# Layer one of a feed-forward block as seven block products instead of eight, on one Trainium2 core

## The chip, the cores and the metric

The kernel runs on one core of one Trainium2 chip. The metric is the device time of one execution in microseconds, as the median of the runs listed below. Five engines of the core work side by side: TensorE (PE in the profile; its weight loads are shown as PEld), VectorE (DVE), ScalarE (ACT), GpSimd (POOL) and SyncE (SP), which here issues every DMA.

## The reference

Attention over 8 sequences with 8 heads (32 global tokens and 512 local ones per sequence, head size 64), then layer norm and a feed-forward block with a residual. Cut to what matters:

```python
# out_g: every global query sees all keys
# out_l: a local query sees 32 keys to either side and the global keys
x = concatenate([out_g, out_l], axis=2).transpose(0, 2, 1, 3).reshape(8, 544, 512)
mu, var = mean(x), mean((x - mu) ** 2)            # over the last axis
xn = (x - mu) / sqrt(var + 1e-6) * g_ln
out = x + maximum(xn @ w_ch1, 0.0) @ w_ch2        # w_ch1: 512 x 2048, w_ch2: 2048 x 512
```

All inputs are fp32 (the weights are given as float64). The kernel gets fp32 accuracy out of matmuls on a rounded format, fp32r, by splitting each operand into a high part and a low rest, and adding three products: low by high, high by low, high by high.

## The kernel before

The 4352 tokens are worked in nine chunks. Chunks 0 to 7 hold 512 local tokens each (two halves of 256 tokens, each a half of one sequence), chunk 8 the 256 global tokens. Within a chunk the feed-forward block runs over 16 row tiles `f` of 128 hidden units each:

- `hidden(f)` (L804) is layer one of a row tile: three products times four contraction tiles `kt` of 128, so 12 matmuls of 512 columns, all into one PSUM bank `ph`.
- `relu` (L815, ACT) writes the high part `hh` out of `ph`, `rest` (L819, DVE) the low part `hl`.
- `out(f, t)` (L831) is layer two: for each of four token tiles `t` three matmuls of 512 columns, added up in PSUM over all 16 row tiles (`acc`). The outputs of row tile `f` stand behind `hidden(f + 1)`. At the end of a chunk DVE adds the residual (L863) and SP stores (L864).

The split weights of all 16 row tiles, high and low, of both layers, stay in SBUF from chunk 0 on (`wts`).

The attention of later chunks is put between these matmuls. `attend(u, before)` issues the scores of one pair of heads `u` (L454), the values of the pair before (L522), the masked row maxima (L472, DVE), the exponentials (L487, ACT), and turns the 32x32 blocks of the result on DVE (L413). `PAIR_PLACES` and `GLOBAL_PLACES` say behind which half row tile each piece starts. The pieces are generators in a queue `side`; each call of `step()` between two groups of matmuls moves the first one on to its next `yield`. What is issued so is in the fixed order of each engine's queue: nothing overtakes anything on its engine. After the last pair of a half of a chunk, DVE takes the statistics (L236), GpSimd the power (L243), ACT normalises (L252), DVE turns the tokens (L413), and `split_chunk` scales them by `g_ln` into high parts (L761, ACT) and low rests (L763, DVE).

GpSimd has little to do behind chunk 0: for each attention pair an addition and a power on 8 columns (L534, L536), for each half the norm's power.

Of the kernel before, what the change touches and what calls it, by code (L numbers as in the profile page):

```python
# [21 lines left out]
P = 128  # L22
# [48 lines left out]
PAIR_PLACES = (4, 10, 18, 24)  # L71
GLOBAL_PLACES = (1, 7, 20)
# [3 lines left out]
REBIAS = 2.0 ** -112  # L76
HUGE = 122877.9921875 * REBIAS
# [6 lines left out]
def attention_ffn_kernel(  # L84
# [82 lines left out]
    wts = {}  # L167
# [3 lines left out]
    class Weights:  # L171
# [42 lines left out]

        def high(self):
            w = wpool.tile([P, 2, KT * P + DM], F32R, name="w", tag=f"w{self.f}")
            wts[self.f] = w[:, 0], w[:, 1]
            nc.scalar.copy(w[:, 0], self.tmp)  # L218

        def low(self):  # L220
            hi, lo = wts[self.f]
            nc.vector.tensor_tensor(lo, self.tmp, f32(hi), op=ALU.subtract)  # L222

    class Norm:
# [46 lines left out]
        def steps(self):  # L271
            self.stats()
            self.power()
            yield
            self.shift()
# [7 lines left out]
    def new_x():  # L283
        return fpool.tile([P, 2, DM], F32, name="x", tag=next(xtags))
# [135 lines left out]
    class Pair:  # L420
# [135 lines left out]
        def norm(self):  # L556
            half = self.at[2]
            xn = ready.setdefault(self.chunk, [None, None])[half] = new_x()
            return Norm(token_tile(self.chunk, half), range(2), xn)

    class Global:
# [39 lines left out]
        def reduce(self, part):  # L601
            if part == 0:
                self.p = fpool.tile([P, 2, SA], F32, name="gp", tag="ob")
# [34 lines left out]
        def turns(self, half):  # L638
# [4 lines left out]
            for n in range(4 * half, 4 * half + 4):  # L643
                turn_blocks(p, self.pt, n)
                yield
# [94 lines left out]
    def split_chunk(xns, turns, out):  # L740

        def source(h, kt):
            if h in turns:
                return turns[h].rearrange("p j (k q) -> p j k q", k=KT)[:, :, kt]
            t = ps_a.tile([P, 512], F32, name="t", tag="att")
            for j in range(2):
                at = slice(j * P, (j + 1) * P)
                nc.tensor.transpose(t[:, at], xns[h][:, j, kt * P:(kt + 1) * P], ident)
            return t[:, :256].rearrange("p (j q) -> p j q", j=2)

        for kt in range(KT):
            planes(kt, out, len(xns) > 1)
            parts = [
                (source(h, kt), *(
                    a[:, h * 256:(h + 1) * 256].rearrange("p (j q) -> p j q", j=2) for a in out[kt]
                ))
                for h in range(len(xns))
            ]
            g = g_sb[:, kt:kt + 1]
            for t, hi, lo in parts:  # L760
                nc.scalar.activation(hi, t, AF.Copy, scale=g)  # L761
            for t, hi, lo in parts:
# [488 lines left out]
```

## Time and profile before

| | |
|---|---|
| median of 3 runs | 899.88 us (898.98 to 900.23) |
| profiled execution, its own time | 898.62 us |
| its span, first to last instruction | 896.8 us |
| TensorE busy | 880.2 us (98%) |
| VectorE busy | 626.0 us (70%) |
| ScalarE busy | 301.6 us (34%) |
| GpSimd busy | 112.7 us (13%) |
| DMA moved | 119.28 MB, mean 133 GB/s |

Busy times are sums over the span. The profiled execution takes 1.8 us more than its span, and 1.3 us less than the median of the runs.

### The profile page before, as it was taken

Reading aid. Unit: us, or ns where it says so; the run is one execution under the profiler, and the core shown is the slowest. Engines: PE = TensorE matmul, PEld = TensorE weight load, DVE = VectorE, ACT = ScalarE, POOL = GpSimd, SP = SyncE. Lnnn points to the kernel's source line nnn. Section 1 sums busy time; section 2 is a strip of 40 time slices with the busy share of each in tenths; the row PEclk is TensorE's granted clock in tenths of the full one; section 3 lists DMA queues with packets and bytes.
Section 4 is the critical chain, followed back from the end, with each engine's and each line's share of the span. In section 5 each row is a group of like instructions: output and inputs, shape, how many; then the busy total and the mean of one; then the engine's idle time right before and its main releaser. Section 6 shows DMA issues by size and latency. Waiting matters only on the chain.

```text
span 896.8 us, 20638 instructions
## 1 busy us (share of the span) xinstructions
PE 880.2 (98%) x8492; PEld 702.7 (78%) x8492; DVE 626.0 (70%) x1765; ACT 301.6 (34%) x843; POOL 112.7 (13%) x152
## 2 busy tenths in 40 slices
PE   6899999999999999999999999999999999999998
PEld 4777777788777887788877887878877787777897
DVE  6886835878868786787958786888958775342611
ACT  7876754323233233323232232323332212111211
POOL 5731221101011000111011000010011000000000
PEclk9999999999999999999999999999999999999999
DMA  9992448323253243423253243423263123302100
GB/s 352 417 419 72 164 127 302 126 74 122 109 187 102 79 149 126 157 64 128 108 211 102 80 148 104 157 74 125 103 232 102 48 72 99 120 0 63 50 21 23
DMA packets 48109, 119.28 MB, mean 133 GB/s; under 512 B 4240, under 2 KB 15504, under 8 KB 44944
## 3 DMA queue, kind: packets, MB, share of 16 engines
q1 hardware_dynamic: 48016, 117.98, 37.3%
q8 instruction: 66, 1.08, 0.5%
q14 instruction: 27, 0.22, 0.1%
HBM read 100.14 MB, written 17.83 MB: 132 GB/s over the span
## 4 chain that ended last, share of the span: by engine, by line
PE 91%; DMA 5%; ACT 1%; DVE 1%; SPq 0%; issue 0%; ACTq 0%
PE ph L804 41%; PE acc L831 41%; DMA raw<-in_wd 3%; PE sc L454 3%; PE pv L522 3%; DMA u<-in_eu 2%; PE gsc L653 1%; PE gsc L591 1%; DVE w L222 1%; ACT p L487 0%; PE pv L653 0%; PE tp L502 0%; DVE tmp L211 0%; ACT w L218 0%; PE t L700 0%
## 5 line engine op out<-in xcount | busy, mean ns | idle before, releaser
L831 PE MATMUL acc<-w,hh 128*128 128x512 f32 x1088 | 342.2, 396 | 0.0
L804 PE MATMUL ph<-xh,w 128*128 128x512 f32 (+1 forms) x1240 | 310.4, 377 | 1.5 <-DVE hl L819 1.5
L804 PEld LDWEIGHTS ph<-xh,w 128*128 128x128 f32 x1240 | 216.5, 188 | 49.2 <-DVE hl L819 2.5
L831 PEld LDWEIGHTS acc<-w,hh 128*128 128x128 f32 x1088 | 204.8, 188 | 48.2
L815 ACT ACTIVATE hh<-ph 128x512 fp32r<-128x512 f32 (+1 forms) x147 | 83.2, 566 | 438.4 <-PE ph L804 433.4
L831 PE MATMUL acc<-w,hl 128*128 128x512 f32 x544 | 216.9, 399 | 0.0
L819 DVE SCALAR_TENSOR_TENSOR hl<-ph,hh 128x512 fp32r<-128x512 f32 (+1 forms) x147 | 95.6, 651 | 164.9 <-ACT hh L815 163.4
L413 DVE STREAM_TRANSPOSE pt<-p 32x256 f32<-32x256 f32 x368 | 160.3, 435 | 5.2
L804 PE MATMUL ph<-xl,w 128*128 128x512 f32 (+1 forms) x524 | 141.1, 391 | 0.0
L831 PEld LDWEIGHTS acc<-w,hl 128*128 128x128 f32 x544 | 102.1, 188 | 24.1 <-issue 0.6
L487 ACT ACTIVATE p<-p,mn 128x128 f32<-128x128 f32 x224 | 87.3, 391 | 93.2 <-DVE mn L472 89.8
L804 PEld LDWEIGHTS ph<-xl,w 128*128 128x128 f32 x524 | 97.3, 188 | 23.1
L413 DVE STREAM_TRANSPOSE x<-x 32x256 f32<-32x256 f32 x208 | 90.7, 436 | 6.2 <-ACT x L252 3.2
L472 DVE CUSTOM_DVE_ANT_0 p<-sc,mask 128x128 f32<-128x128 f32 x224 | 51.2, 286 | 49.2 <-PE sc L454 49.2
L413 DVE STREAM_TRANSPOSE gpt<-gp 32x256 f32<-32x256 f32 x128 | 55.5, 434 | 1.8
L536 POOL TENSOR_TENSOR ri<-ri,powers 128x8 f32<-128x8 f32 x29 | 49.8, 1716 | 2.4
L487 ACT ACTIVATION_READ_ACCUMULATOR p<-p,mn 128x1 f32 x224 | 41.9, 187 | 0.0
L242 POOL TENSOR_SCALAR rs<-mv 128x2 f32<-128x2 f32 x17 | 4.8, 281 | 258.6 <-DVE mv L238 258.5
L534 POOL TENSOR_SCALAR ri<-sm 128x8 f32<-128x8 f32 x29 | 7.4, 256 | 205.1 <-ACT p L487 204.2
L454 PEld LDWEIGHTS sc<-e 64*32 64x32 f32 x1792 | 24.9, 105 | 9.8 <-issue 9.2
L454 PE MATMUL sc<-e 64*32 64x128 f32 x1792 | 32.4, 274 | 0.0
L522 PEld LDWEIGHTS pv<-v,pt 128*32 128x32 f32 x1792 | 26.3, 110 | 6.0 <-issue 6.0
(90 smaller groups left out, 523.9 us busy)
## 6 DMA issues: line engine op xcount, KB each, us to landing
v<-in_eu SPq DMA_DIRECT2D x28, 1024.0 KB, 7.3
e<-in_eu SPq DMA_DIRECT2D x28, 672.0 KB, 8.1
raw<-in_wd SPq DMA_DIRECT2D x16, 1024.0 KB, 15.5
gk<-in_gk SPq DMA_DIRECT2D x8, 1088.0 KB, 8.0
ob<-xs SPq DMA_DIRECT2D x34, 256.0 KB, 7.1
out<-ob SPq DMA_DIRECT2D x34, 256.0 KB, 2.2
xs<-x SPq DMA_DIRECT2D x32, 256.0 KB, 8.6
gv<-in_gv SPq DMA_DIRECT2D x16, 512.0 KB, 4.4
```

Source lines behind the costliest of these rows:

```text
L222: nc.vector.tensor_tensor(lo, self.tmp, f32(hi), op=ALU.subtract)
L413: nc.vector.transpose(out=to[rp][..., gp], in_=a[gp][..., rp])
L454: nc.tensor.matmul(sc[h][gp, at:at + P], self.e[hd, j, w * WIN:(w + 1) * WIN], self.e[hd, j, k0 * WIN:(k0 + 4) * WIN], start=True, stop=Tr ...
L472: nc.vector.tensor_tensor_reduce(out=self.p[:, j, c], in0=self.sc[h][:, at:at + P], in1=masks[self.at[2], qb], scale=-QSCALE, scalar=BIG, ...
L487: nc.scalar.activation(self.p[:, j, c], self.p[:, j, c], AF.Exp, bias=self.mn[:, j, c:c + 1], scale=-1.0, accum_out=self.sm[:, j, c:c + 1],)
L522: nc.tensor.matmul(self.pv[gp, at:at + D], self.pt[:, j, 2 * h + qb, gp], self.v[:, j, 4 * qb + g, h * D:(h + 1) * D], start=True, stop=Tr ...
L536: nc.gpsimd.tensor_tensor(ri, ri, minus_one.to_broadcast([P, 8]), op=ALU.pow)
L591: nc.tensor.matmul(banks[h][i * SG:(i + 1) * SG, :c1 - c0], self.q[h * D:(h + 1) * D, i, :], self.k[h * D:(h + 1) * D, i, c0:c1], start=Tr ...
L804: nc.tensor.matmul(ph[:, :n], w[:, kt, :], xx[kt][:, part.start:part.start + n], start=(i == 0), stop=(i == 3 * KT - 1),)
L815: nc.scalar.activation(hh[:, :n], self.ph[f, start][:, :n], AF.Relu)
L819: nc.vector.scalar_tensor_tensor(hl[:, :n], self.ph[f, start][:, :n], 0.0, f32(hh[:, :n]), ALU.max, ALU.subtract)
L831: nc.tensor.matmul(self.acc[t], a[:, ts], w, start=(f == 0 and i == 0), stop=(f == NF - 1 and i == 2),)
```

## The change

For chunks 2 to 7, layer one of two neighbouring row tiles (a pair `p` of row tiles: 256 hidden units) is made by seven block products in place of eight. The weights of the pair are cut into 2x2 blocks (128 hidden units by 256 contraction rows), the tokens into 2x2 blocks (256 contraction rows by 256 tokens). Sums and differences of weight blocks and of token blocks take the place of some blocks, and the four result blocks are sums of products. Layer two is computed as before.

- `Sums.sums`, `high`, `low` and `store`, run by `prepare` during chunk 1: GpSimd makes four sums of weight blocks for each of the 8 pairs, ACT and GpSimd split them into high and low, and SP stores all eight blocks of each pair to a DRAM tile `wb` (`Weights.store` the plain ones). `prepare` is moved on once at each of four places per row tile of chunk 1; it has 53 steps.
- `load_blocks(p, True)` loads the seven blocks of a pair back, for each pair of each chunk, in four DMAs, into places that the layer-one weights of row tiles 0 to 7 held; pairs with even numbers have one set of places, odd ones the other. The blocks of pair `p + 2` are loaded as soon as pair `p` has used its own. Chunk 8 loads the four plain blocks of a pair (`load_blocks(p, False)`).
- `pair` replaces two calls of `hidden`: 42 matmuls of 256 columns into three half banks `x`, `y` and `w`. A running sum stays in `x`: product 2 is added to product 0 there, then 4, then 6. Between them ACT copies the partial sums out (`s1`, `s7`, `s6`, `s2`, `s5`, `s4`), GpSimd adds pairs of these copies, and `relu` and `rest` follow for four blocks, three of the rests on GpSimd. The layer-two matmuls of the pair before stand between the products and behind them: `FILLS` gives one token tile ahead of products 2, 4 and 6 each, and five follow product 6.
- The last layer-two outputs of a chunk are carried into the next chunk's first pair (`carried`).
- `turn_half` scales the turned tokens by `g_ln` (ACT), `token_sums` makes four sums of token blocks (GpSimd), and `split_blocks` splits seven token blocks of 128x512 into high (ACT) and low (DVE). They take the place of `split_chunk`.
- The attention pairs move to other places, and their GpSimd power is issued behind their own exponentials; the two halves of a pair's row maxima are issued together.

The first chunk keeps its order, chunk 1 keeps `hidden`. The diff, cut:

```diff
-PAIR_PLACES = (4, 10, 18, 24)
-GLOBAL_PLACES = (1, 7, 20)
+FILLS = (0, 0, 1, 0, 1, 0, 1)
+STAGE_AT = 4
+PAIR_PLACES = ((2, 8, 15, 21), (2, 7, 14, 18, 30), (6, 14, 18, 30))
+GLOBAL_PLACES = ((29, 31, 31), (22, 31, 31))
...
+        def sums(self):
+            pool, tag = ((apool, "gk"), (fpool, "ob"))[self.p % 2]
+            ab = apool.tile([P, 2, KT * P], F32, name="wf", tag="gp")
+            for i in range(2):
+                w = f32(wide[2 * self.p + i][:, :, :KT * P])
+                nc.gpsimd.tensor_tensor(ab[:, i], w[:, 0], w[:, 1], op=ALU.add)
+                yield
+            a, b = ab[:, 0], ab[:, 1]
+            self.s = pool.tile([P, 4, 2, KH], F32R, name="ws", tag=tag)
+            self.lo = f32(self.s[:, :, 1])
+            for n, (i, x, y, op) in enumerate((
+                (2, b[:, :KH], b[:, KH:], ALU.add),
+                (1, self.lo[:, 2], a[:, :KH], ALU.subtract),
+                (0, a[:, :KH], b[:, :KH], ALU.subtract),
+                (3, a[:, KH:], self.lo[:, 1], ALU.subtract),
+            )):
+                nc.gpsimd.tensor_tensor(self.lo[:, i], x, y, op=op)
...
+    def load_blocks(p, seven):
+        for n, at in enumerate(
+            (slice(0, 2), slice(2, 4), slice(4, 6), slice(6, 7)) if seven
+            else (slice(0, 4, 3), slice(5, 8, 2))
+        ):
+            blocks = wb[p][at].rearrange("b p l c -> p b (l c)")
+            nc.sync.dma_start(
+                f32(wide[p % 2 * 4 + n])[:, :blocks.shape[1], :KT * P], blocks
+            )
...
+        for n, a, b in (
+            (0, x[0, 1], x[0, 0]), (2, x[1, 1], x[0, 1]), (1, x[1, 1], t[0]), (3, x[1, 0], t[1]),
+        ):
+            nc.gpsimd.tensor_tensor(t[n], a, b, op=ALU.subtract)
+            yield
...
+        for n, a in enumerate((x[0, 0], t[2], t[1], x[1, 0], t[0], t[3], x[1, 1])):
...
+            nc.scalar.copy(as_block(hi), a)
+            nc.vector.tensor_tensor(as_block(lo), a, as_block(f32(hi)), op=ALU.subtract)
...
+        def pair(self, p, fill):
...
+            def product(i, to, start=True, stop=True):
+                a, b = block_at(p, i), self.xt[i]
+                for n, (l, r) in enumerate(((a[1], b[0]), (a[0], b[1]), (a[0], b[0]))):
+                    for k in range(KB):
+                        nc.tensor.matmul(
+                            to, l[:, k * P:(k + 1) * P], r[:, k * KH:(k + 1) * KH],
...
+            fill(0)
+            product(0, x, stop=False)
+            nc.scalar.copy(s1, x)
+            fill(1)
+            product(1, w, stop=False)
+            nc.scalar.copy(s7, w)
+            fill(2)
+            product(2, x, False, False)
+            nc.scalar.copy(s6, x)
+            fill(3)
+            product(3, y, False, False)
+            nc.scalar.copy(s2, y)
+            add(s1, s2)
+            fill(4)
+            product(4, x, False, False)
+            nc.scalar.copy(s5, x)
+            add(s5, s7)
+            fill(5)
+            product(5, w, False)
+            nc.scalar.copy(s4, w)
+            add(s6, s4)
+            relu(0, 0, s1)
+            rest_pool(0, 0, s1)
+            fill(6)
+            product(6, x, False)
+            relu(0, 1, x)
+            rest(0, 1, x)
+            relu(1, 1, s5)
+            rest_pool(1, 1, s5)
+            relu(1, 0, s6)
+            rest_pool(1, 0, s6)
+            fill(7)
...
+        for kt in range(KT):
+            nc.scalar.activation(x[:, :, kt], x[:, :, kt], AF.Copy, scale=g_sb[:, kt:kt + 1])
+            if kt % 2:
                 yield
+        if len(halves) == 2:
+            yield from token_sums(u.chunk)
+            summed.add(u.chunk)
```

How the change moves instructions is shown at three places. First TensorE, in the middle of chunk 5. Before, a row tile of layer one (`ph`, 12 matmuls) and behind it the first of the four token tiles of layer two of the row tile before (`acc`):

```order
L804 MATMUL ph<-xh_6328,w 128x512 x2
L804 MATMUL ph<-xh_6344,w 128x512 x2
L804 MATMUL ph<-xl_6329,w 128x512 x2
L804 MATMUL ph<-xl_6345,w 128x512 x2
L804 MATMUL ph<-xh_6328,w 128x512 x2
L804 MATMUL ph<-xh_6344,w 128x512 x2
L831 MATMUL acc_6498<-w,hl 128x512
L831 MATMUL acc_6498<-w,hh 128x512 x2
```

And in the changed kernel, pair 3 of chunk 5, with an attention pair (`sc`, `pv`) behind it:

```order
L1031 MATMUL ph<-xb,w 128x256 x6
L1031 MATMUL ph<-w 128x256 x6
L956 MATMUL acc_7603<-w 128x512 x3
L1031 MATMUL ph<-w 128x256 x6
L1031 MATMUL ph<-xb,w 128x256 x6
L956 MATMUL acc_7622<-w 128x512 x3
L1031 MATMUL ph<-w 128x256 x12
L956 MATMUL acc_7645<-w 128x512 x3
L1031 MATMUL ph<-w 128x256 x6
L528 MATMUL sc<-e 32x128 x32
L596 MATMUL pv<-v,pt_7778 32x64 x32
```

Two row tiles of layer one, 24 matmuls of 512 columns, have become seven products of six matmuls of 256 columns, and three of the eight layer-two tiles of the pair before stand between them. Over the whole program 1152 matmuls of 512 columns are gone and 2016 of 256 columns are there instead; the 1632 of layer two stay.

Second ScalarE, the same part of a chunk. Before, exponentials (`p`), the ReLU that makes `hh`, and the normalisation (`x<-x,rs`):

```order
L815 ACTIVATE hh<-ph 128x512 x3
L487 ACTIVATE p_6800,sm_6805<-p_6800,mn_6799 128x128 x8
L815 ACTIVATE hh<-ph 128x512
L252 ACTIVATE x<-x,rs 128x512 x2
L815 ACTIVATE hh<-ph 128x512 x3
```

And in the changed kernel, around one pair of row tiles that follows an attention pair (`sn` are the copied sums, `w` here the places that take the high part of the hidden units, `x<-x,g_sb` the scaling of turned tokens):

```order
L561 ACTIVATE p_8068,sm_8073<-p_8068,mn_8067 128x128 x8
L1055 COPY sn<-ph 128x256
L1058 COPY sn<-ph 128x256
L1061 COPY sn<-ph 128x256
L1254 ACTIVATE x<-x,g_sb 128x2x128 x2
L1064 COPY sn<-ph 128x256
L1254 ACTIVATE x<-x,g_sb 128x2x128 x2
L1068 COPY sn<-ph 128x256
L1072 COPY sn<-ph 128x256
L1039 ACTIVATE w<-sn 128x256
L1039 ACTIVATE w<-ph 128x256
L1039 ACTIVATE w<-sn 128x256 x2
```

Where two ReLUs of 512 columns stood, there are now six copies and four ReLUs of 256 columns, and other work of ScalarE stands between the copies.

Third GpSimd, the start of chunk 1. Before, the power of an attention pair and little else:

```order
L534 TENSOR_SCALAR ri_1826<-sm_1812 128x8
L536 TENSOR_TENSOR ri_1826<-ri_1826,powers 128x8
L630 TENSOR_SCALAR gsm<-gsm 128x2
L534 TENSOR_SCALAR ri_2116<-sm_1812 128x8
L536 TENSOR_TENSOR ri_2116<-ri_2116,powers 128x8
```

In the changed kernel (`wf` are whole weights, high plus low, `ws` the four sums of a pair):

```order
L248 TENSOR_TENSOR wf<-w 128x512 x2
L259 TENSOR_TENSOR ws<-wf 128x256
L259 TENSOR_TENSOR ws<-ws,wf 128x256
L259 TENSOR_TENSOR ws<-wf 128x256
L259 TENSOR_TENSOR ws<-wf,ws 128x256
L248 TENSOR_TENSOR wf<-w 128x512 x2
L608 TENSOR_SCALAR ri_2091<-sm_2070 128x8
L610 TENSOR_TENSOR ri_2091<-ri_2091,powers 128x8
L269 TENSOR_TENSOR ws<-ws 128x2x256
```

Each of the 8 pairs brings two additions of 512 columns, four sums of 256 and two subtractions of 512 to GpSimd in chunk 1.

## Rows read from the trace of the kernel before

**Rows 1.** The page: span, and busy time of each engine.

```profile
span 896.8 us, 20638 instructions
PE 880.2 (98%) x8492; PEld 702.7 (78%) x8492; DVE 626.0 (70%) x1765; ACT 301.6 (34%) x843; POOL 112.7 (13%) x152
```

**Rows 2.** The page: chain that ended last, share of the span by engine.

```profile
PE 91%; DMA 5%; ACT 1%; DVE 1%; SPq 0%; issue 0%; ACTq 0%
```

**Rows 3.** Windows: stretch, length, busy us of PE PEld DVE ACT POOL, PEclk, DMA share, GB/s.

```profile
230.00:330.00 100.00, 100.00 (x1003) 79.52 (x1002) 78.71 (x230) 30.62 (x96) 9.75 (x13) 1.00 0.36 125
```

**Rows 4.** Waits of the whole span: who waited for whom, us, times, longest.

```profile
ACT hh L815 <- PE ph L804: 433.4, 127, 7.6
...
PE ph L804 <- DVE hl L819: 1.5, 2, 0.8
```

**Rows 5.** The chain in order of time, chunk ends: start us, us, what.

```profile
339.41 5.62 PE acc L831 x24
...
441.03 5.62 PE acc L831 x24
```

**Rows 6.** Timeline, weight loads in chunk 3: start us, us, what.

```profile
407.50 0.89 PEld L804 LDWEIGHTS ph<-xh,w 128*128 128x128 f32 x4
...
410.31 0.19 PEld L831 LDWEIGHTS acc<-w,hl 128*128 128x128 f32 x1
...
413.12 0.89 PEld L804 LDWEIGHTS ph<-xh,w 128*128 128x128 f32 x4
```

**Rows 7.** Timeline, start of chunk 8, whose layer one has 256 columns.

```profile
846.97 3.06 PEld L804 LDWEIGHTS ph<-xh,w 128*128 128x128 f32 x24
847.20 3.04 PE L804 MATMUL ph<-xh,w 128*128 128x256 f32 x24
...
850.08 0.39 PE L831 MATMUL acc<-w,hl 128*128 128x512 f32 x1
...
850.28 0.39 ACT L815 ACTIVATE hh<-ph 128x256 fp32r<-128x256 f32 x1 [1.06 <-PE ph L804]
```

**Rows 8.** Groups by line and form: count, busy us, mean ns, idle before.

```profile
L815 ACT ACTIVATE hh<-ph 128x512 fp32r<-128x512 f32 x125 | 74.9, 599 | 395.7 <-PE ph L804 390.7 <-PE acc L831 4.7
...
L252 ACT ACTIVATE x<-x,rs 128x512 f32<-128x512 f32 x30 | 22.8, 809 | 13.4 <-DVE rs L246 13.4
...
L761 ACT ACTIVATE xh<-x,g_sb 128x256 fp32r<-128x256 f32 x52 | 21.5, 498 | 0.0
...
L815 ACT ACTIVATE hh<-ph 128x256 fp32r<-128x256 f32 x22 | 8.3, 383 | 42.7 <-PE ph L804 42.7
```

**Rows 9.** Groups of GpSimd by line and form.

```profile
L536 POOL TENSOR_TENSOR ri<-ri,powers 128x8 f32<-128x8 f32 x29 | 49.8, 1716 | 2.4
L197 POOL TENSOR_SCALAR raw<-raw 128x1024 int32<-128x1024 uint16 x5 | 16.7, 3342 | 9.7 <-DMA raw<-in_wd 9.4
...
L534 POOL TENSOR_SCALAR ri<-sm 128x8 f32<-128x8 f32 x29 | 7.4, 256 | 205.1 <-ACT p L487 204.2
...
L200 POOL TENSOR_SCALAR tmp<-tmp 128x1024 f32<-128x1024 f32 x2 | 2.1, 1068 | 8.1 <-ACT tmp L185 8.1
```

**Rows 10.** Windows of 4 us in which the DMA engines were nearly full.

```profile
258.00:262.00 4.00, 4.00 (x18) 3.21 (x18) 1.98 (x8) 2.01 (x9) 1.91 (x2) 1.00 1.00 389
...
322.00:326.00 4.00, 4.00 (x19) 3.24 (x18) 3.37 (x10) 2.51 (x6) 0.94 (x2) 1.00 0.94 295
```

**Rows 11.** DMA issues of the page: KB each, median us from issue to landing.

```profile
v<-in_eu SPq DMA_DIRECT2D x28, 1024.0 KB, 7.3
e<-in_eu SPq DMA_DIRECT2D x28, 672.0 KB, 8.1
```

**Rows 12.** Timeline of an attention pair of chunk 3.

```profile
399.91 1.16 PE L454 MATMUL sc<-e 64*32 64x128 f32 x64
...
401.44 0.40 ACT L487 ACTIVATE p<-p,mn 128x128 f32<-128x128 f32 x1 [3.62 <-DVE mn L472]
...
404.70 0.19 ACT L487 ACTIVATION_READ_ACCUMULATOR p<-p,mn 128x1 f32 x1
```

More of the change, by code (lines that the diff above doesn't have):

```diff
@@ L764, in split_chunk, with step @@
             yield
     out_flat = out.rearrange("b s d -> (b s) d")
-    side, first = deque(), deque()
-    def step():
-        for queue in (first, side):
-            while queue:
-                if next(queue[0], queue) is not queue:
+    side, ends, later = deque(), deque(), deque()
+    held = {}
+    def step(free=1, queues=(side, later, ends)):
+        for queue in queues:
+            while queue and held.get(queue[0], 0) <= free:
+                got = next(queue[0], queue)
+                if got == "wait":
+                    break
+                if got is not queue:
+                    held[queue[0]] = got or 0
@@ L893, in attention_ffn_kernel @@
     weights = [Weights(f) for f in range(NF)]
+    sums = [Sums(p) for p in range(NP)]
     ready, tokens = {}, {}
@@ L896, in attention_ffn_kernel @@
     halves_turned = {}
+    summed = set()
     def token_tile(c, half):
         if (c, half) not in tokens:
-            tokens[c, half] = new_x()
+            tokens[c, half] = new_x((c, "token"))
         return tokens[c, half]
@@ L904, in attention_ffn_kernel, with prepare, attend @@
     acm, apool = open_pool("apool")
-    def accumulators():
-        return [ps_o.tile([P, 512], F32, name="gsc", tag=f"acc{t}") for t in range(4)]
-    def attend(u, before):
+    def prepare():
+        for p in range(NP + 1):
+            s, before = sums[p] if p < NP else None, sums[p - 1] if p else None
+            steps = s.sums() if s else iter(())
+            for n in range(4):
+                if n % 2 == 0 and before:
+                    before.high(n // 2)
+                next(steps, None)
+                yield
+                if n % 2 and before:
+                    before.low(n // 2)
+                    yield
+            if p:
+                before.store()
+            if p == NP - 1:
+                globals_[0].load_scores()
+            for w in weights[2 * p:2 * p + 2]:
+                w.store()
+        yield
+    def attend(u, before, late=False):
         if u:
@@ L916, in attend @@
             before.values()
-            before.sums()
             if before.next:
@@ L966, in attend_global @@
+    def attend_global(g, before, tag="gq"):
+        g.scores(0, [ps_a.tile([P, 512], F32, name="sc", tag="att") for _ in range(2)])
+        banks = [ps_h.tile([P, 512], F32, name="gsc", tag="ph") for _ in range(2)]
+        before.values(banks[0][:, P:2 * P])
+        g.scores(1, banks)
         g.reduce(0)
         g.reduce(1)
-        if before:
-            before.output()
+        before.output(tag)
         g.load_values()
-        if g.next:
-            g.next.load_scores()
+        yield
+        for h in range(2):
+            g.exps(h)
+            yield
@@ L973, in attend_global, with first_global @@
+    def first_global(g):
+        g.scores(0, [ps_a.tile([P, 512], F32, name="sc", tag="att") for _ in range(2)])
+        yield
+        g.scores(1, [ps_h.tile([P, 512], F32, name="gsc", tag="ph") for _ in range(2)])
+        g.reduce(0)
+        g.reduce(1)
+        g.load_values()
         yield
```

392 lines of the change are left out of this document (279 added, 113 removed).

## The prediction

> **What bounds the kernel now.** The page's busy shares come first: TensorE is busy in 880.2 of 896.8 us [rows 1]. That alone proves little, since ends of matmuls are modelled, so the chain that ended last is read next: 91% of the span lies on TensorE, 5% on DMA (the start) [rows 2]. The window of 100 us in the middle shows no idle TensorE at a granted clock of 1.00, that is 2.4 GHz, while VectorE works 78.7, ScalarE 30.6 and GpSimd 9.8 us and the DMA engines are filled to 0.36 [rows 3]. The waits agree: ScalarE waits 433 us for layer one, TensorE in layer one 1.5 us for others [rows 4]. So from chunk 1 on the time is the sum of what TensorE issues, and 101.6 us per chunk (339.41 to 441.03) [rows 5]. Fewer matmul columns shorten the run, as long as nobody else gets late.
>
> **TensorE's part.** The pace of a matmul is read from start to start. Twelve loads of 512-column matmuls go from 407.50 to 410.31, the next twelve to 413.12: 2.81 us each, 0.234 per matmul [rows 6]. In chunk 8 layer one already has 256 columns: 24 matmuls from 847.20 to 850.08, 0.120 each [rows 7]. A pair of row tiles took 24 x 0.234 = 5.62 us and takes 42 x 0.120 = 5.04, so 0.58 less; 48 pairs (8 in each of chunks 2 to 7) give 27.8 us. The work in multiplications falls by an eighth, the time by a tenth, since a matmul of 256 columns costs more than half of one of 512. Bounds: below, half of 0.234, 0.117, which gives 4.92 and 33.8 us in all; above, the loads' own row, 3.06 us for 24, 0.1275 each [rows 7], which gives 5.36 and 12.8 us. I take 0.120, a start-to-start time of the same shape, with the loads in that stretch back to back. The gain is gone at 5.62 / 42 = 0.134.
>
> In that stretch the weight loads have no gap (3.06 us of loads within 2.99 us, 846.97 to the next block's) [rows 7]. The Trainium skill, "TensorE: Matmul & The Clock Gate", section "LDWEIGHTS (loading the stationary operand)", has a load take its columns divided by 1.2 ns, 107 ns for 128. By that alone, as an estimate, a pair would take 4.5 us and the run about 848; the row's 0.120 is 12% slower, and I follow the row.
>
> **The chain within a pair.** A product takes 0.72 us, a layer-two tile 3 x 0.234 = 0.70, a pair of row tiles 7 x 0.72 + 8 x 0.70 = 10.64. Products 0, 2, 4 and 6 go into the same bank, and each must wait until ScalarE has copied the sum before. From the end of a 256-column group (850.08, the next starts) to ScalarE's start are 0.20 us, and it works 0.39 [rows 7]: a copy is done 0.59 behind its product. Between products 0 and 2 stand product 1 and a tile, 1.42 us; between 2 and 4, and 4 and 6, likewise. So each has 0.83 us to spare. The first pair of a chunk has no tile ahead of product 6, there 0.13 are left. What eats the spare time is what stands between the copies on ScalarE. Scaling by g costs 0.498 a piece [rows 8]: with two behind s6 and two behind s2, counted from product 2's end, the copies end at 0.59 (s6), 1.98 (s2) and 3.36 (s5), and product 6 wants s5 at 3.56. With four behind s2, s5 ends near 3.7, 0.1 late. A normalisation (0.809) stands behind s5, where nobody waits soon. The eight exponentials behind an attention pair run from 401.44 to 404.89, that is from 1.5 to 5.0 us after the scores began (399.91) [rows 12]; the next first copy is due more than 6 us after the scores begin (2.1 of attention, five tiles of 3.5, one product), so they fit. I book 0.3 us per chunk for such misses, and 1 us for the handover from chunk 1, together 3 us.
>
> **ScalarE and VectorE in sum.** A pair brings ten ScalarE operations of 0.39 for two of 0.60 [rows 8], 2.7 us more, 22 us per chunk on top of 30.6; scaling and casts of tokens add about 4. That is 57 of 97 us. VectorE loses three of four rests. Neither becomes the bound.
>
> **GpSimd.** No row shows a plain two-input addition. The nearest arithmetic is a multiply by 1024 columns at 1068 ns (1.04 ns per column), and a converting one at 3342 (3.26) [rows 9]; the powers (1716 ns for 8 columns) are two-input forms too, but a power, and I leave them out as a price for an addition. I take the middle, 2.1 ns. Chunk 1: 3072 columns per pair, 24,576 in all, 26 to 80 us, 52 as taken; four attention pairs add 4 x 1.97 = 7.9. The 53 steps of 64 places last 53/64 x 101.6 = 84 us. So it fits at 60, and at 88 it is 4 us late. In each later pair six two-input and three one-input operations of 256 columns cost 4.0 us (at most 7.5) of 10.64, and their results are wanted a whole pair later. Price taken: nothing, hidden under 10.64 us of TensorE; up to 16 us if slow (below).
>
> The Trainium skill, "GPSIMD Engine Reference", section 3.1, gives 4497 ns for such an addition of 2048 columns, 2.2 ns each; by it, as an estimate, the sums take 54 us and the forecast stays. No run here shows it yet.
>
> **DMA.** A pair loads 7 blocks of 0.262 MB, 1.84 MB, a chunk 14.7 MB. When the engines were nearly full they moved 389 GB/s, or 295 at a share of 0.94 (314 if full) [rows 10]: 38 to 47 us per chunk. The present traffic fills 0.36 x 101.6 = 37 us [rows 3]. So 75 to 84 of 97 us: busy, not full. Chunk 1's 16.8 MB of stores come out alike. A pair's load has from the last product of its places to their next use five tiles and a pair, 14.2 us (16.3 across an attention pair); by the 7.3 us of a 1.05 MB load [rows 11], scaled, it needs 12.8. Price taken: nothing.
>
> **Sum.** The profiled execution took 898.6, the median is 1.3 higher; 899.9 - 27.8 + 3 = 875.1. Differences under 0.2% (1.8 us) can't be told from none here.
>
> **The rivals.**
> - Columns set the pace alone, 0.117 per matmul: 899.9 - 33.8 + 3 = 869. For it: nothing but the ratio; against it: the row. Chance 0.05.
> - GpSimd is slow (3.26 ns). Chunk 1 ends 4 us late, and the four token sums of 512 columns ahead of each of five later chunks take 6.7 us in place of 4.3; ScalarE's casts wait for them with the copies behind, 5 x 2.4 = 12. Together 16: 880 to 891. GpSimd's near empty row [rows 1] speaks against it, the missing price for it. Chance 0.14. The Trainium skill, "GPSIMD Engine Reference", section 4.1, advises VectorE for elementwise work on a tile, which goes this way.
> - The copies miss their 0.83 us in nearly every pair, by 0.4 to 0.7 us, because ScalarE or GpSimd holds the queue: 48 x 0.5 = 24, so 892 to 906, about no change. Against it: the spare time as counted. Chance 0.09.
> - Slower: weights come late. Where an attention pair's 1.7 MB (e and v [rows 11]) stand ahead in the queue, they cost 5.9 us at 295 GB/s, so 12.8 + 5.9 = 18.7 against 16.3, 2.4 late, at the 20 attention pairs of chunks 2 to 6: 48 us, near 923. It decides from 1.25 us per such pair on (25 / 20). Against it: those loads are issued behind the weights, and the engines have 13 us per chunk left. Chance 0.08.
> - The rest, among it the same matmul time without any gain, 0.04.
>
> **How the numbers follow.** The forecast, 871 to 879 (no to 7 us of waits), has 0.60. Faster: 0.60 + 0.05 + 0.14, 0.04 of the third case and 0.02 of the rest, 0.85; same: 0.02 + 0.01; slower: 0.08, 0.03 of the third case, 0.01 of the rest, 0.12. The range takes in the forecast, the columns' rival nearly whole, GpSimd's, and the lower edge of the third: 868 to 895, 0.8.
>
> **What would show it.** Right: a window of 100 us in chunks 3 to 6 with TensorE still at 100 and a chunk of about 97 us; product groups of six 0.72 us apart; ScalarE near 57 and GpSimd near 45 us per 100. Wrong: TensorE waiting for ScalarE's copies at products 2, 4, 6 (third rival), for the loads of block weights (fourth), ScalarE waiting for GpSimd in chunk 1 or at chunk ends (second), or product groups 0.77 apart (0.1275 per matmul), which leaves 890.

## The result and the profile after

The changed kernel takes 875.95 us (median of 4 runs, 874.95 to 877.99) against 899.47 before (4 runs, 898.98 to 900.23): a ratio of 0.9741, 95% interval 0.9719 to 0.9762. The forecast's sum was 875.1, its range 868 to 895. The profiled execution took 875.12.

The page first: busy times over the span, and the chain that ended last.

```profile
span 873.3 us, 24214 instructions
PE 854.4 (98%) x9356; PEld 732.0 (84%) x9356; DVE 610.7 (70%) x1711; ACT 437.1 (50%) x1285; POOL 481.4 (55%) x670
...
PE 81%; DMA 9%; POOL 4%; DVE 3%; ACT 1%; SPq 1%; issue 1%; POOLq 0%; ACTq 0%
```

TensorE is still what the chain runs on, but with 81% where it was 91% [rows 2]. The other engines have filled up: GpSimd from nearly empty [rows 1] to 55%. The ten points lie between 168 and 269 us: there the chain runs over GpSimd's sums of weights, their stores, the loads and VectorE into a wait of chunk 2, while TensorE is itself busy nearly all the time. Behind 269 us the chain is TensorE's but for about 1%. Where the engines have filled up, the windows of chunks 1 to 3 show (columns as in [rows 3], with counts of instructions in brackets).

```profile
142.00:243.00 101.00, 100.79 (x935) 79.87 (x934) 72.12 (x211) 41.35 (x119) 71.56 (x75) 1.00 0.87 300
243.00:340.00 97.00, 94.30 (x1253) 82.64 (x1252) 81.00 (x230) 52.24 (x169) 59.93 (x86) 1.00 0.89 314
340.00:437.00 97.00, 96.77 (x1153) 85.41 (x1152) 78.39 (x223) 51.63 (x167) 61.65 (x89) 1.00 0.81 281
```

In chunk 3 TensorE is busy in 96.77 of 97 us (chunks 4 and 5 read the same) at a granted clock of 1.00, beside a DMA share of 0.81 (0.36 before [rows 3]). In chunk 2 it misses 2.70 us. The chain in order of time gives the pace, in a pair in the middle of a chunk, from 414.85, and in the first pair of one, from 438.71 (columns: start, us, what).

```profile
414.85 1.44 PE ph L1031 x12
416.29 0.69 PE acc L956 x3
416.98 1.43 PE ph L1031 x12
...
421.95 3.43 PE acc L956 x15
425.37 1.44 PE ph L1031 x12
...
435.08 3.63 PE acc L956 x15
438.71 1.65 PE ph L1031 x12
...
441.06 1.67 PE ph L1031 x12
...
532.32 3.63 PE acc L956 x15
```

In the middle twelve matmuls take 1.43 to 1.44 us, 0.120 each, and a tile 0.69 to 0.70: the numbers of [rows 6, 7], in another place. The first pair of a chunk loses 0.45 us (1.65 and 1.67 for 1.44 and 1.43). The same piece stands at the end of two chunks, at 435.08 and at 532.32: 97.24 us per chunk, where [rows 5] gave 101.6. Taken for five chunks, the 0.28 over 101.6 - 4.64 and the 2.70 of chunk 2 are 4.1 us; 899.9 - 27.8 + 4.1 = 876.2. So the sum closes, but only in net. The pair from 414.85 to 425.37, with no attention behind it, takes 10.52 us. Two row tiles without attention took 11.21 before, from the first of these pieces to the second:

```profile
364.04 2.80 PE ph L804 x12
...
375.25 1.09 PE sc L454 x64
```

That is 0.69 us less per pair, not 0.58: 0.60 in layer one (5.01 for 5.61) and 0.09 in layer two (5.51 for 5.60), whose matmuls are the same as before. Why these run a little faster now is not shown. For 48 pairs it makes 33 us instead of 27.8. The waits are larger than booked by about as much: 0.45 us in the first pairs of chunks 3 to 6 (1.8 in all), 0.48 in the last pairs of chunks 2 to 5 (13.33 where other pairs with the same attention take 12.85; 1.9 in all), the 2.7 of chunk 2, and 1.2 at the handover (the first product of chunk 2 starts at 241.61 with 2.81 us of chunk 1's layer two still to come, where before chunk 2 started at 243.26 with none left). Of the 33 these 7.6 leave 25.4; the result is 23.5, and the other 2 us are not taken apart.

The last pair's wait, in chunk 3 (timeline: start, us, engine, line, what; in brackets the idle time ahead and who ended it):

```profile
429.63 0.62 ACT L867 CAST w<-ts 128x512 fp32r<-128x512 f32 x1 [0.81 <-POOL ts L848]
430.16 0.36 ACT L1064 COPY sn<-ph 128x256 f32<-128x256 f32 x1
430.57 0.98 PE L1031 MATMUL ph<-w 128*128 128x256 f32 x6 [0.23 <-ACT sn L1064]
```

The sixth product waits for the fourth one's copy (L1064), the copy stands on ScalarE behind a cast of the next chunk's tokens (L867), and the cast waits for a token sum of GpSimd (L848). In the first pair of chunk 4 the second product starts 0.15 us late, and its weights are loaded just behind the end of a VectorE instruction (438.52 + 0.74 = 439.26):

```profile
438.52 0.74 DVE L616 TENSOR_TENSOR x<-pv,ri 128x256 f32<-128x256 f32 x2
...
439.38 0.78 PEld L1031 LDWEIGHTS ph<-w 128*128 128x128 f32 x6
```

L616 reads the attention's values (`pv`) out of one of the two PSUM banks that the products use too. The 0.12 us between the two is 0.11 and 0.12 in chunks 3 and 5, and in chunk 7, whose first pair follows no attention pair, nothing is late. So the first group most likely waits for VectorE; no experiment tested it.

What the sum does not tell is how much room the other engines have left. The experiments were chosen for that.

GpSimd's new groups, by form (mean ns of one behind the busy time; then the idle time ahead of them, and for what).

```profile
L1046 POOL TENSOR_TENSOR sn<-sn 128x256 f32<-128x256 f32 x144 | 112.0, 783 | 149.7 <-ACT sn L1064 107.1 <-ACT sn L1068 21.9 <-ACT sn L1072 19.9
L1051 POOL TENSOR_TENSOR w<-sn,w 128x256 fp32r<-128x256 f32 x144 | 106.3, 738 | 12.0
L1050 POOL TENSOR_SCALAR sn<-sn 128x256 f32<-128x256 f32 x144 | 62.2, 432 | 0.1
...
L269 POOL TENSOR_TENSOR ws<-ws 128x512 fp32r<-128x512 f32 x16 | 20.6, 1293 | 2.8 <-ACT ws L265 2.8
```

A pair costs GpSimd 3 x 0.783 + 3 x 0.738 + 3 x 0.432 = 5.9 us.

### The profile page after: what moved, and what is told of

It reads as the page before. It is cut to its first block, busy times and chain, and to the rows that moved or that the text cites. A ratio compares the mean times of both kernels' runs of the same rounds, so it can differ in the third digit from the quotient of the medians.

```text
span 873.3 us, 24214 instructions
## 1 busy us (share of the span) xinstructions
PE 854.4 (98%) x9356; PEld 732.0 (84%) x9356; DVE 610.7 (70%) x1711; ACT 437.1 (50%) x1285; POOL 481.4 (55%) x670
## 4 chain that ended last, share of the span: by engine, by line
PE 81%; DMA 9%; POOL 4%; DVE 3%; ACT 1%; SPq 1%; issue 1%; POOLq 0%; ACTq 0%
PE acc L956 38%; PE ph L1031 27%; PE ph L927 7%; PE sc L528 3%; PE pv L596 3%; DMA u<-in_eu 3%; DMA raw<-in_wd 2%; DMA wb<-ws 2%; POOL ws L259 2%; DMA e<-in_eu 2%; PE gsc L729 1%; POOL ws L269 1%; PE sc L665 1%; POOL wf L248 1%; DMA w<-wb 1%; DVE pt L487 1%
## 5 line engine op out<-in xcount | busy, mean ns | idle before, releaser
L956 PE MATMUL acc<-w 128*128 128x512 f32 x1164 | 300.7, 395 | 0.0
L956 PEld LDWEIGHTS acc<-w 128*128 128x128 f32 x1164 | 206.2, 189 | 34.9 <-POOL w L1051 0.3
L1031 PEld LDWEIGHTS ph<-w 128*128 128x128 f32 x1440 | 193.8, 190 | 16.9 <-issue 1.8
L1031 PE MATMUL ph<-w 128*128 128x256 f32 x1440 | 203.3, 283 | 2.9 <-DVE x L616 2.0
L1046 POOL TENSOR_TENSOR sn<-sn 128x256 f32<-128x256 f32 x144 | 112.0, 783 | 149.7 <-ACT sn L1064 107.1
L1051 POOL TENSOR_TENSOR w<-sn,w 128x256 fp32r<-128x256 f32 x144 | 106.3, 738 | 12.0
L561 ACT ACTIVATE p<-p,mn 128x128 f32<-128x128 f32 x224 | 86.9, 391 | 38.2 <-DVE mn L546 38.2
L956 PE MATMUL acc<-w,hh 128*128 128x512 f32 x312 | 98.1, 396 | 0.0
L927 PEld LDWEIGHTS ph<-xh,w 128*128 128x128 f32 x472 | 74.7, 188 | 13.9 <-DVE hl L944 2.1
L956 PEld LDWEIGHTS acc<-w,hh 128*128 128x128 f32 x312 | 58.9, 189 | 12.6
L956 PE MATMUL acc<-w,hl 128*128 128x512 f32 x156 | 63.5, 407 | 0.0
L1043 DVE SCALAR_TENSOR_TENSOR w<-ph,w 128x256 fp32r<-128x256 f32 x48 | 20.2, 422 | 58.5 <-ACT w L1039 58.0
```

The lines of the kernel that those rows point to most:

```text
L561: nc.scalar.activation(self.p[:, j, c], self.p[:, j, c], AF.Exp, bias=self.mn[:, j, c:c + 1], scale=-1.0, accum_out=self.sm[:, j, c:c + 1],)
L927: nc.tensor.matmul(ph[:, :n], w[kt], xx[kt][:, part.start:part.start + n], start=(i == 0), stop=(i == 3 * KT - 1),)
L956: nc.tensor.matmul(self.acc[t], a[:, ts], w, start=(f == 0 and i == 0), stop=(f == NF - 1 and i == 2),)
L1031: nc.tensor.matmul(to, l[:, k * P:(k + 1) * P], r[:, k * KH:(k + 1) * KH], start=(start and n == k == 0), stop=(stop and n == 2 and k == K ...
L1046: nc.gpsimd.tensor_tensor(z, z, b, op=ALU.add)
L1051: nc.gpsimd.tensor_tensor(hl, z, f32(hh), op=ALU.subtract)
```

## The experiments

Twelve kernels, each an edit of the changed one. Times are medians; for comparison the changed kernel's 875.95, and 898.9 to 899.4 for the kernel before on the same chips. An edit that adds lines moves the line numbers behind it by one to three, so that L1051 can be L1052 in its rows. In the profiled runs chunk 2 starts between 241.3 and 243.8 us (244.6 with a load done twice), also where an edit touches nothing ahead of it, so a difference of 2 us in a total is not read as an effect.

**One more product.**

```
 fill(0)
 product(0, x, stop=False)
+product(0, x, stop=False)
```

> Edit: the first of the seven products of every pair is run twice (it starts its sum anew, so the values stay as they are): six more matmuls of 256 columns in each of 48 pairs, nothing else. If TensorE's columns set the pace of chunks 2 to 7: 48 x 6 x 0.120 = 34.6 us more, 910 to 911 us, above the kernel before. If copies, GpSimd or the loads set it and TensorE only looks full: 876 to 890 us.

905.71 us (905.39 to 907.49), ratio 1.0074 (1.0059 to 1.0089): 29.8 more. Pairs in the middle take what was said: the first product of one pair and of the next stand at 401.49 and 414.85 in the changed kernel, and at 408.63 and 422.70 here, 14.07 for 13.36, 0.71 more. The rest went into idle time that was there anyway: the window of chunk 2 misses 1.25 us instead of 2.70, and a chunk is 5.4 us longer, not 5.76, since the last pairs no longer wait for the copy L1064. The first pair is longer by the whole 0.71 (11.68 for 10.97). With this one product the whole gain is gone. The columns do set the pace.

**One product fewer.**

```
 fill(6)
-product(6, x, False)
```

> Edit: the seventh product of a pair is left out (one block of layer one's sums lacks a term, so the output is not the reference's); the other work stays. If TensorE's columns set the pace: 34.6 us less, 841 us, or 30 less as the eighth product cost, 846. If GpSimd, ScalarE or the loads are close behind (GpSimd's last block of a pair is ready late when it has 3.4 us more): the gain stops earlier, 850 to 870 us.

859.43 us (858.67 to 860.19): 16.5 less, half of 34.6. A stretch of one chunk's length, in windows:

```profile
433.00:528.00 95.00, 92.57 (x1106) 79.19 (x1105) 77.69 (x227) 51.57 (x168) 62.00 (x90) 1.00 0.83 289
```

TensorE now misses 2.4 us of 95, and the chain through chunk 4, grouped by line, has turned: the transposes of attention on VectorE lead it, and TensorE is no longer among its first lines.

```profile
by line: DVE pt L487 33.8%; DVE x L487 11.4%; ACT p L561 11.3%; issue 10.6%; DVE gpt L487 9.9%; DVE p L546 5.6%; DVE ob L969 4.9%; DVE x L616 2.4%; DVE st L305 2.3%; DVE w L1043 2.1%; ACT w L1039 1.9%; ACT x L321 1.5%; ACT sn L1055 0.6%; AC
```

So VectorE, whose share the forecast had passed over, stands a few per cent behind TensorE: not by its sum (77.7 of 95) but by the order in its queue.

**No tiles between the products.** Two forms. In the first, the steps of attention and norms that go with the tiles moved along.

```
-FILLS = (0, 0, 1, 0, 1, 0, 1)
+FILLS = (0, 0, 0, 0, 0, 0, 0)
```

> Edit: no tile of layer two is put between the seven products of a pair; all of the pair before's stand behind them. If a copy really ends 0.59 us after its product while the product in between takes 0.72 us: no change, 874 to 880 us. If the tiles between are what hides the copies (each copy delayed by other work on ScalarE): TensorE waits 0.3 to 0.7 us at four products of a pair, 48 pairs, 930 to 1010 us.

935.87 us (934.06 to 936.50), 60 more. That looks like the second theory, but the timeline shows something else.

```profile
378.99 7.14 DVE L487 STREAM_TRANSPOSE pt<-p 32x256 f32<-32x256 f32 x16
...
386.16 0.16 DVE L315 SCALAR_TENSOR_TENSOR rs<-mv,rs 128x2 f32<-128x2 f32 x1
386.36 0.81 ACT L321 ACTIVATE x<-x,rs 128x512 f32<-128x512 f32 x1 [5.03 <-DVE rs L315]
387.08 0.35 ACT L1064 COPY sn<-ph 128x256 f32<-128x256 f32 x1
...
387.48 2.93 PE L1031 MATMUL ph<-w 128*128 128x256 f32 x12 [5.13 <-ACT sn L1064]
```

A norm's application (L321) now stands ahead of a copy (L1064) on ScalarE. It needs L315 on VectorE, which stands behind sixteen transposes of 0.44 us. ScalarE waits 5.03 us with the copy behind it, and TensorE 5.13. There are eight such waits, 28 us. After this one twelve matmuls take 2.93 us instead of 1.44: in the window of 387 to 392 us the granted clock was 0.50, the lower of its two levels (1.2 and 2.4 GHz), which is part of the other 32. In pairs without such a wait the 42 matmuls in a row take 5.16 us, 0.12 above 7 x 0.72 (0.15 above the 5.01 of the changed kernel). The second form keeps the steps in place:

```
 for i in range(FILLS[n] if left and n < 7 else 0):
-    left.popleft()()
     if n < 6:
         step(0)
...
+for _ in range(sum(FILLS) if left else 0):
+    left.popleft()()
 n = len(left)
```

> Edit: the three tiles of layer two that stand between the products of a pair are put behind the seventh, as in the run before, but the steps of attention, norm and token work stay where they were between the products. In the run before, 42 products in a row took 5.16 us where nothing else was moved, against 7 x 0.72 = 5.04. If copies keep pace without the tiles and the loss of 60 us came from a norm's work that was moved ahead of a copy on ScalarE: 48 x 0.12 = 6 us more, 878 to 885 us. If the tiles are what hides the copies: still above 920 us.

889.71 us (889.10 to 890.86): 13.8 more, between the two. The chain tells both parts of it:

```profile
443.63 0.74 PE ph L1031 x6
...
444.83 1.54 ACT p L561 x8
446.37 0.26 ACT sn L1058
...
446.68 3.18 PE ph L1031 x24
...
455.33 5.17 PE ph L1031 x42
```

In an ordinary pair the row of 42 costs 0.13 us over 7 x 0.72, and the pair 0.10 more than in the changed kernel (10.63 for 10.53), 5 us over 48 pairs. In the first pair of a chunk four exponentials (L561) stand between the first two copies on ScalarE (L1055, L1058). From 444.37 to 446.68 TensorE does two products, 1.44 us, and waits 0.87 for the second copy; the four products behind take 3.18 instead of 2.88. That is 1.2 us where the changed kernel loses 0.45; the whole pair takes 11.69 for 10.97, in chunks 3 to 6 2.9 us in all. Their fifth pair is longer by 0.8 as well (13.65 for 12.84), 3.2 in all: in chunk 4 its chain runs over scalings of tokens (L1255), which stand on ScalarE between the third product's copy and the fifth's. The rest of the 13.8, 3 to 4 us, lies in chunks 2 and 6 and is not traced. The tiles between the products hide the copies' latency, as the prediction has it, but in an ordinary pair they hide little. What makes the copies late is other work ahead of them in ScalarE's queue.

**The exponentials later.** If they cost the first pair 0.45 us, they can be moved. The edit is the step in which an attention pair goes on; first behind the fifth product's copy (a), then behind the second's (b).

```
 if n < 6:
-    step(n % 2 * 2)
+    step(2 if n == 5 or n % 2 and p else 0)        (a)
+    step(2 if (n % 2 if p else n > 1) else 0)      (b)
```

> Edit: in the first pair of a chunk, the second half of an attention pair's exponentials on ScalarE stands behind the fifth product's copy instead of ahead of the second's. In the changed kernel the first three product groups of a chunk take 1.65, 1.67 and 2.15 us instead of 1.44, 1.44 and 2.15. If these exponentials are the cause: 4 chunks x 0.45 us = 1.8 us less, 873 to 875 us. If the copies' delay is not on the path, or VectorE, which turns what they make, gets late in their place: no change, 875 to 877 us.

898.33 us (896.73 to 899.36), ratio 0.9982 (0.9973 to 0.9990): nearly the whole gain is lost by one step in another place. The second product group is fast now (1.43), but 20 us later the timeline reads:

```profile
464.48 6.29 DVE L487 STREAM_TRANSPOSE gpt<-gp 32x256 f32<-32x256 f32 x14
...
470.80 0.42 DVE L1043 SCALAR_TENSOR_TENSOR w<-ph,w 128x256 fp32r<-128x256 f32 x1
471.28 0.98 PE L1031 MATMUL ph<-xb,w 128*128 128x256 f32 x6 [2.03 <-DVE w L1043]
```

The exponentials start 9.12 us behind the chunk's last tiles (451.17, 442.05), where it was 4.72 (439.80, 435.08): VectorE can begin its transposes of them 4.4 us later, and the rest of a seventh product (L1043) stands behind fourteen of the next ones. TensorE waits 2.03 us for it and soon after 1.46 for L616, all in all 16.5 us for VectorE, and the granted clock of 473 to 477 us was 0.63. A chunk takes 102.49 us. The second trial:

> Edit: the same exponentials stand behind the second product's copy, one copy later than in the changed kernel, where the run before had put them three copies later. Counted from the end of the second product, the second copy ends at 0.59 us, the exponentials at 2.14, the third product's copy at 2.53, and the fifth product wants it at 2.84. If the first three product groups of a chunk were slow because of these exponentials, and the 22 us of the run before came from VectorE, which got what they make 3 us later: 4 chunks x 0.45 us = 1.8 us less, 873 to 875 us. If any delay of the exponentials makes VectorE late: 878 to 898 us. If the slow groups have another cause: 875 to 877 us.

880.23 us (877.03 to 881.13; three of its five runs at 880 to 881, two at 877), ratio 0.9779 (0.9760 to 0.9797). Not faster than the changed kernel, and rather slower. The second group was cured as worked out (1.43), the first was not (442.14 1.67 x12 in the chain), which fits its wait for L616: there too the weights are loaded 0.12 us behind its end. The first pair gains 0.24 us (10.73 for 10.97), but the third and the fourth lose 0.2 and 0.6 (10.73 and 13.47 for 10.53 and 12.84). VectorE gets the exponentials 0.9 us later (444.10 behind 438.51), and a norm's L315, which stands behind its transposes of them, is later too. On ScalarE the norm's application (L321) stands ahead of the third pair's last copy and waits for L315, 3.79 us where it is 3.03 in the changed kernel, and the rest of the seventh product (L1043) follows late:

```profile
475.09 0.82 ACT L321 ACTIVATE x<-x,rs 128x512 f32<-128x512 f32 x1 [3.79 <-DVE rs L315]
...
476.78 0.43 DVE L1043 SCALAR_TENSOR_TENSOR w<-ph,w 128x256 fp32r<-128x256 f32 x1 [1.73 <-ACT w L1039]
...
477.26 0.98 PE L1031 MATMUL ph<-w 128*128 128x256 f32 x6
```

A chunk takes 97.80 us there (the pieces at 438.51 and 536.31), 0.56 more. So the place of the exponentials is a bargain between TensorE's first pair (0.2 us) and VectorE's queue (more).

**More work on GpSimd.** Each relu block's clamp and rest twice (a), and only the last block's (b).

```
+for _ in range(2):                                    (a)
     nc.gpsimd.tensor_scalar(z, z, LARGEST, 0.0, ALU.min, ALU.max)
     nc.gpsimd.tensor_tensor(hl, z, f32(hh), op=ALU.subtract)
...
 rest_pool(1, 0, s6)
+rest_pool(1, 0, s6)                                   (b)
```

> Edit: GpSimd does the clamp and the rest of each of its three relu blocks of a pair twice (same values): 3 x (0.40 + 0.73) = 3.4 us more per pair, 27 us more per chunk, 89 of 97 us busy. If GpSimd is hidden as long as it fits in the chunk: 875 to 880 us. If its chain behind the products is on the path: 3.4 us per pair, 163 us more, 1039 us; if only the block that the next pair's third product overwrites comes late: about 1 us per pair, 924 us.

932.26 us (931.17 to 933.10): 56 more. The granted clock over the run is 0.981, against 0.995, so a part of that is the clock behind long waits. The wait itself is this one:

```profile
497.70 0.37 ACT L1062 COPY sn<-ph 128x256 f32<-128x256 f32 x1 [4.33 <-POOL w L1052]
498.12 1.70 PE L1031 MATMUL ph<-w 128*128 128x256 f32 x12 [2.30 <-ACT sn L1062]
```

The third product's copy writes the sum s6 that GpSimd reads last in the pair before. The deadline of GpSimd's chain is that copy, not the use of its results. TensorE waits for it in 15 places, 28.1 us. In the longest (3.49 us at 551.44, in the last pair of a chunk) the copy stands behind a cast (L867) that has waited 4.83 us for the token sums (L848), which GpSimd starts late.

> Edit: GpSimd does the clamp and the rest of only the last of its three relu blocks of a pair twice (same values), 1.13 us more per pair instead of 3.4. The 3.4 us cost 56 us / 48 = 1.2 us per pair. If GpSimd has a fixed spare time of 3.4 - 1.2 = 2.2 us per pair: hidden, 875 to 879 us. If every us on GpSimd costs its share (contention, or a chain without spare time): 0.4 us per pair, 19 us more, 894 us.

889.19 us (888.14 to 890.31): 13.2 more, so neither theory. A chunk takes 99.6 us, and TensorE waits for that same copy (L1061) in 9 places, 7.8 us, the longest 1.0. Chunk 3 has two of them, 0.82 us at 384.35 and 0.99 at 435.18. Ahead of the first GpSimd had stood idle for 3.36 us: it waited for the last copy of its pair (L1072), which stands on ScalarE behind a norm's application (L321) that waited 3.03 us for VectorE. At the second the copy itself stands behind a cast (L867) that waited 2.33 us for the next chunk's token sums (L848, four of 1.5 us from 431.21, behind GpSimd's longer chain). So it is not the share of every pair: where another queue has already made a chain late there is no room for 1.13 us, and the other pairs hide it.

**The loads' place in the queue.**

```
 self.pair(p, fill)
-q = p + 2
-load_blocks(q % NP, ...)
...
     left.popleft()()
...
+q = p + 2
+load_blocks(q % NP, ...)
```

> Edit: the loads of weight blocks are issued behind the five tiles that follow a pair, so that an attention pair's loads, where there are some, stand ahead of them in the queue. If the forecast's estimate holds (12.8 us for a pair's blocks, 5.9 us for the attention loads ahead, 16.3 us of time): 2.4 us late at 20 pairs, 48 us, near 923 us. If the blocks land about as fast as the trace shows (a median of 5 us each, the four side by side): no change, 874 to 880 us.

906.41 us (903.81 to 907.98), ratio 1.0079 (1.0059 to 1.0098): 30 more, and slower than before the change. The DMA queue's timeline (start, time in issuing and waiting) of this kernel,

```profile
457.06 11.13 SPq L970 DMA_DIRECT2D out<-ob  x4
468.28 3.08 SPq L289 DMA_DIRECT2D w<-wb  x4
...
472.81 0.38 SPq L510 DMA_DIRECT2D e<-in_eu  x1
...
476.71 10.53 SPq L289 DMA_DIRECT2D w<-wb  x8
```

and of the changed one:

```profile
448.05 1.96 SPq L289 DMA_DIRECT2D w<-wb  x4
451.52 7.20 SPq L970 DMA_DIRECT2D out<-ob  x3
...
460.47 2.38 SPq L289 DMA_DIRECT2D w<-wb  x4
462.94 0.63 SPq L510 DMA_DIRECT2D e<-in_eu  x1
```

The chunk's first product starts at 448.00 in the one and at 438.54 in the other. Behind it the loads for the third pair (the first x4) are issued after 20.3 us and after 9.5, those for the fourth after 28.7 and 21.9. Now the stores of outputs (L970), each of which waits for a tile that VectorE has to finish, stand ahead of the first, and the attention pair's loads ahead of the second. TensorE waits for weights in both pairs, 1.77 us and then 3.75:

```profile
488.27 1.62 PE L1031 MATMUL ph<-xb,w 128*128 128x256 f32 x6 [3.75 <-DMA w<-wb]
```

In the window of 488 to 492 us the granted clock was 0.50. In all there are seven waits for weights, 18.4 us; the clock behind them goes with the rest of the 30 us. The mechanism is the forecast's rival, at fewer places, and with the outputs' stores as a second cause.

**Loads earlier.** Each load right behind the product that frees its tile:

```
 nc.scalar.copy(s7, w)
+load(0)
...
 add(s1, s2)
+load(1)
...
 add(s6, s4)
+load(2)
```

> Edit: each of the four loads of weight blocks is issued right behind the product that frees its tile, up to 5 us earlier, instead of all four behind the seventh product. If loads are late only in chunk 2, where TensorE is idle 2.7 of 97 us: 873 to 876 us, with chunks 3 to 7 unchanged at 97.2 us. If loads hold back every pair a little: below 871 us.

875.63 us (874.86 to 877.32), ratio 0.9738 (0.9723 to 0.9753): no change, and chunk 2's window still misses 2.74 us. Its waits say why: TensorE waits there for VectorE (L616 2.0 us, L1043 0.5), not for a load. The first theory had the place right and the cause wrong.

**More traffic.** One load twice into the same tile, and the same bytes copied to a place that nobody uses:

```
-for n, at in enumerate((...)):
+for n, at in parts[:1] * seven + parts:                                  (a)
...
+if seven:                                                                (b)
+    nc.sync.dma_start(next(scrap), wb[p][:2].rearrange("b p l c -> b p (l c)"))
```

> Edit: one of the four block loads of a pair (512 KB) is done twice, 4.2 MB more per chunk: 31.5 MB, 81 us at 389 GB/s, of 97. If the DMA engines are no bound as long as they fit in the chunk: 874 to 880 us. If loads are already nearly late: 0.5 to 1.5 us per pair, 900 to 945 us.

> Edit: behind the four block loads of a pair, 512 KB of blocks are also copied from DRAM to a place in DRAM that nobody reads and nothing waits for: 4.2 MB more read per chunk, as in the run that loads one part twice, but without the wait of the second load for the first. If that run's 86 us came from the queue that stood at this wait, and not from traffic: 81 of 97 us at 389 GB/s, so 875 to 885 us. If the traffic itself is what the loads can't stand: above 920 us.

(a) 962.44 us (961.43 to 966.66), 86 more; (b) 880.37 us (879.81 to 881.38), 4.4 more. The bytes are the same, 257.96 MB on both pages. A stretch of one chunk's length in windows, of (a) and then of (b):

```profile
470.00:580.00 110.00, 99.38 (x1211) 87.32 (x1216) 79.61 (x225) 52.48 (x170) 62.64 (x91) 0.95 0.82 292
```

```profile
437.00:535.00 98.00, 96.15 (x1138) 84.45 (x1122) 77.50 (x224) 50.91 (x166) 60.60 (x89) 1.00 0.87 320
```

With (b) the DMA engines are fuller (0.87 against 0.82) and TensorE misses 1.85 of 98 us. In (a) the second load into a tile must wait until the first has landed, and the queue stands for that with everything behind it: over the run it waits 361.9 us for blocks to land, in (b) 20.2. In (a) TensorE waits 31.1 us for the queries and keys of attention (e), 10.5 for its values, 10.2 for the global keys, and only 5.2 for blocks. So (a) did not test what it was built for; (b) did, but for one thing: its extra bytes go to DRAM and not into SBUF, and what landing them there would cost is not shown.

## Why the prediction was right, point by point

- **TensorE, 27.8 us less.** Right in what sets the pace, low in the sum: 0.120 per matmul held in every product group away from the chunks' first and last pairs, and one product added cost 0.71 per pair. But a pair takes 0.69 us less and not 0.58, since layer two, booked as unchanged, takes 0.09 less: 33 us. The loads came no faster than the row had said: the Trainium skill, "TensorE: Matmul & The Clock Gate", section "LDWEIGHTS (loading the stationary operand)", divides a load's columns by 1.2, which is 107 ns for 128; here twelve matmuls with a load each take 1.43 us, 0.120, and the measurement decides.
- **3 us for misses and the handover.** Too little: the 33 us and the measured 23.5 leave over 9, with up to 0.9 instead of 0.3 per chunk in first and last pairs, 2.7 in chunk 2, for which there was no term, and 1.2 at the handover, booked as 1. The 0.28 per chunk over 101.6 - 4.64 looks like the 0.3 only because layer two's gain hides the rest. The gain is 5 us larger than booked and the waits are 6 to 7 us longer. That the result lies within 1 us of the sum is therefore partly luck; that it lies in the range is not.
- **The chain of copies, 0.83 us to spare.** Right in ordinary pairs. Without any tile 0.13 was to be left per product; measured, seven in a row take 5.17 instead of 5.04, so the copies just miss. In the first pair the trouble was foreseen at the seventh product and came at the first four, part of it from exponentials between two copies. In the last pair it came at the sixth product, from a cast between two copies, for which the sum had no term.
- **GpSimd, price nothing.** Nearly right on the time, wrong on two terms. At 2.1 ns per column a fixed part was missing: 256 columns take 0.74 us and 512 take 1.29, that is 2.15 ns per column and 0.19 on top. So a pair cost 5.9 us, not 4.0, a chunk 61.6, not 45, and chunk 1's sums about 65 (16 of 1.29 twice, 32 of 0.74), not 52. The Trainium skill, "GPSIMD Engine Reference", section 3.1, has 4497 ns for an addition of 2048 columns, 2.2 ns each, which agrees with the slope. And "wanted a whole pair later" was wrong: the sum s6 is written again three products into the next pair. The rival of a slow GpSimd was therefore nearer than its 0.14 said by the deadline, though the price fell well under its 3.26. What it said of the chunks' ends did come: casts wait for the token sums with a copy behind them, but for 1.9 us in all and not 12.
- **ScalarE 57 us per chunk**: 51.7. **DMA 75 to 84 of 97 us**: 0.81 x 97 = 79. The 12.8 us for a pair's loads was long: the four of a pair land in a median of 5.0 to 5.2 us each.
- **"Neither becomes the bound" of VectorE.** By its sum (78.4 of 97) true, but it is the engine that four experiments ran into, and the idle time of chunk 2 is a wait for it. The forecast looked at sums there where it should have followed the queue.
- **The rival of late weights.** Its mechanism is real and its sign too (906 us when the loads are issued later), but the order in the queue as changed avoids it, and traffic alone costs 4.4 us for 4.2 MB per chunk.

Left open: why layer two's matmuls became a little faster, where some 2 us of the waits lie, and how chunk 2 could be freed of its waits for VectorE. No version tried beats the changed kernel.

## What to carry to other kernels

When a change lightens the busiest engine, add up the others' busy time, but then follow each in-order queue for what stands ahead of the one instruction that the busy engine waits for: here a norm ahead of a copy, fourteen transposes ahead of a rest and a store ahead of a load cost 60, 22 and 30 us, with no engine's work added. A buffer's deadline is the next write to it, not the use of what was made from it. A sum that comes out right can hide two terms that are wrong: compare pair with pair, not only total with total. To price traffic, let it go where nothing waits for it; a load repeated into its own tile prices the queue.

## What the runs showed of the hardware

Some instructions of VectorE and GpSimd hold each other up. In the changed kernel a subtraction of 512 columns on VectorE (L868, two SBUF inputs) takes 0.68 us alone and 0.97 to 1.57 where GpSimd's work overlaps it for 0.6 us or more, and GpSimd's operations of 256 columns, 0.74 and 0.40 alone, take up to 1.20 and 0.84 beside it:

```profile
432.91 2.37 DVE L868 TENSOR_TENSOR w<-ts,w 128x512 fp32r<-128x512 f32 x2
433.54 1.19 POOL L1046 TENSOR_TENSOR sn<-sn 128x256 f32<-128x256 f32 x1
...
434.70 0.84 POOL L1050 TENSOR_SCALAR sn<-sn 128x256 f32<-128x256 f32 x1
```

The Trainium skill, "SBUF — State Buffer", section "SBUF: two separate sides", has the two engines share a pair of ports that one instruction holds for its whole length, also when VectorE has two SBUF inputs; these rows agree.

After waits of 3.75 us (weights) and 5.13 us (a copy) the granted clock was 0.50, 1.2 GHz, for some 6 us (488.3 to 494.1 and 387.5 to 393.5), with twelve matmuls in 2.93 us instead of 1.44. The waits of chunk 2, 0.5 and 1.5 us, left it at 1.00. The pair that follows the wait of 3.75 us has no other wait and takes 15.50 us (488.27 to 503.77) instead of 12.85, so the stall cost another 2.65 us behind its end.
